# Turning half of the first queries behind the first scores, and hashing one pair ahead instead of two

## The chip, the cores and the metric

The kernel runs on one core of a Trainium2 chip. Its time is device time in microseconds (us), from launch to end. The time before is 871.74 us, the median of three runs (871.51 to 871.79). Times inside an execution come from one profiled execution, counted from the start of its span.

The engines of the core have short names in the profile: PE is the matrix engine, PEld its loading of weights, DVE is VectorE, ACT is ScalarE, POOL is GpSimd, and SP is SyncE, which here only issues DMAs. Every engine works through its own queue in order and waits at the head of it.

## What is computed

An attention whose mask comes from a hash, followed by a feed-forward block. The shapes are batch 4, heads 8, sequence 768, head size 64, and for the feed-forward 3072 tokens, 512 wide, 2048 inside. All inputs are 32-bit floats.

```python
# q, k, v: (4, 8, 768, 64); proj: (64, 6)
q_bits = (np.einsum('bhsd,dk->bhsk', q, proj) > 0).astype(np.int64)
k_bits = (np.einsum('bhsd,dk->bhsk', k, proj) > 0).astype(np.int64)
powers = 2 ** np.arange(n_bits)
q_bucket = np.sum(q_bits * powers, axis=-1)
k_bucket = np.sum(k_bits * powers, axis=-1)
mask = q_bucket[:, :, :, None] == k_bucket[:, :, None, :]
scores = scale * np.matmul(q, k.transpose(0, 1, 3, 2))
scores = np.where(mask, scores, -1000000000.0)
scores = scores - np.max(scores, axis=-1, keepdims=True)
attn = np.exp(scores)
attn = attn / (np.sum(attn, axis=-1, keepdims=True) + 1e-09)
attn_out = np.matmul(attn, v)
x = np.ascontiguousarray(attn_out.transpose(0, 2, 1, 3)).reshape(B * S, H * D)   # (3072, 512)
h = x @ w_in                                                                     # (3072, 2048)
g = h * (1.0 / (1.0 + np.exp(-1.702 * h)))
out = g @ w_out                                                                  # (3072, 512)
```

## The kernel before

**Tiling.** The attention works on 16 pairs of heads (`pairs`, numbered n = 0 to 15). The two heads of a pair, j = 0 and 1, lie on the upper and lower 64 partitions. The 768 queries are cut into two halves c = 0 and 1 of 384 (`HS`), and the 768 keys into six tiles of 128 (`kts`: `low` is the first three, `high` the last three, `every` all six).

**The steps of a pair**, with the lines of the kernel before:

- `fetch` (L317) loads k or q in blocks of 32 by 32 with four DMAs on SP's queue, `fetch_v` (L330) loads v with two. k and q have one buffer each, v has two.
- `turn` (L388) makes kT and qT from them, one VectorE transpose each (L391). `measure` (L393) takes the sum of squares on ACT, in the instruction that writes `junk` (L398).
- `hashed` (L402) multiplies kT and qT by the projection on PE, into one bank tagged "m". `featured` (L411) turns the signs into features f on VectorE (L413), and eight small DMAs on SP's queue spread them into kf and qf (L420). kf and qf exist twice, for even and odd pairs.
- `scores(n, c, kts)` (L423): for each key tile, PE adds the product of the features, which masks, to the product of kT and qT (L432), and ACT takes the exponential into e (L433). There are three score buffers in PSUM (`sps`, tag "s").
- `add_low` (L437): POOL adds the first three tiles of e, in two instructions (L440, L441), into acc0, which exists once. `add_high` (L443): VectorE adds the other three tiles and then acc0, in three instructions (L446, L448 twice). `total` (L477): PE sums over the keys (dn, L484).
- `values(n, c, kts)` (L450): PE multiplies e with v into an accumulator av (L463). `unload` (L471): ACT copies it into xT (L474, L475).
- `invert` (L486): VectorE turns dn (rt, L490), takes reciprocals (L493, L497) and turns them back (rs, L499). `norm` (L502): VectorE multiplies xT by them (L504).
- `convert` (L158), driven by `begin` and `step`: from pair 2 on, each pair also converts one chunk of `w_in` from its 64-bit form, with one load (raw, L162), six VectorE instructions (L178 to L198) and one on ACT (L190). The second VectorE step feeds the one on ACT.
- `x_sums`: pairs 12 to 15 each end with one sum over a part of xT on VectorE (L219 to L222), which the feed-forward needs.
- `guard` (L521): in the last pair, the largest of the sums of squares is found, on which a second, slower path depends (L998); with these inputs it is not taken.

**What sets the order.** For PE, VectorE, ACT and POOL the order of the program text is the order on the engine (`ORDERED`, L18). SP's queue is not in that set: a planner places its DMAs when the kernel is built, by its own costs, and each of them waits for its buffer to be free.

**Order around the change.** In `attention` the loop (L559) holds one pair per round. On PE a round is scores of both halves, values of both halves, the hash of pair n + 2 and dn. The keys and queries of pair n + 2 are turned between the two `add_high`, and the features of n + 2 are made after the conversion. k and q of pair n + 3 are fetched behind the first values.

**The first pair** has a path of its own (`first_pair`, L342). It loads its rows in another order and turns on PE: `turned` (L362) makes twelve matmuls with the identity for half of k or q (L366) into a score buffer and copies them out (L368); `bits` (L370) hashes one half on PE (L373) and writes the features on VectorE (L374). The keys' halves are copied by VectorE, the queries' by ACT. All of it comes ahead of the first scores but for the last `bits`, which is returned as `rest` and runs behind the first three score tiles.

**The accumulator av.** For c = 0 it lies in the pool `aps`, which dn uses too. For c = 1 it lies in a score buffer, except in pairs 0, 14 and 15, where it lies in the bank "m" (L454).

**The feed-forward** (from L693) follows with products of a Strassen form and a store of its middle result in DRAM. Its first product's parts are added on VectorE from L735 on.

Of the kernel before, what the change touches and what calls it, by code (L numbers as in the profile page):

```python
# [8 lines left out]
F32 = mybir.dt.float32  # L9
# [10 lines left out]
P = 128  # L20
# [18 lines left out]
def kernel(  # L39
# [17 lines left out]
    nc = tc.nc  # L57
# [10 lines left out]
    HS = HT * P  # L68
# [84 lines left out]
    for x in (0x3FFFFFFF, 0xFF800000):  # L153
        m = const.tile([P, 1], U32, name=f"mask_{x:x}")
# [128 lines left out]
    def attention(ff):  # L283
# [4 lines left out]
        with actx:  # L288
# [53 lines left out]
            def first_pair():  # L342


                b, hp = pairs[0]
                x = {}
                for i, (name, src) in enumerate((("k", k), ("q", q))):
                    raw = raws[0, name] = ld.tile([P, S // 32, 32], F32, tag=name, name=name)
                    x[name] = raw.rearrange("p s i -> p (s i)").rearrange("p (j t d) -> p j t d", j=2, d=D)
                    for j, queue in enumerate((nc.sync, nc.scalar)):  # L350
                        queue.dma_start(out=x[name][:, j], in_=src[b, 2 * hp + j].rearrange("(p t) d -> p t d", p=P))
                    if i == 0:
                        for j, queue in enumerate((nc.sync, nc.scalar)):
                            queue.dma_start(out=pj[D * j : D * (j + 1)], in_=proj)
                    xts[0, name] = wk.tile([P, S], F32, tag=f"{name}T", name=f"{name}T")

                nc.scalar.activation(const.tile([1, 1], F32, name="first"), ones[0:1, 0:1], Act.Exp)
                for _ in range(4):
                    nc.tensor.matmul(aps.tile([P, 512], F32, tag="av", name="warm"), idle[:, 0:P], idle, start=True, stop=True)  # L359
                hash_weights()  # L360

                def turned(name, c, move):  # L362
                    tp = sps.tile([P, 2, 512], F32, tag="s", name="tp")[:, 0, 0:HS]
                    for i in range(GT):
                        for j in range(2):
                            nc.tensor.matmul(tp[D * j : D * (j + 1), i * P : (i + 1) * P], x[name][:, j, c * GT + i, :], ident,  # L366
                                             start=True, stop=True)
                    move(xts[0, name][:, c * HS : (c + 1) * HS], tp)  # L368

                def bits(name, c):  # L370
                    cols = slice(c * HS, (c + 1) * HS)
                    h = sps.tile([P, 2, 512], F32, tag="s", name="hash0")[:, 0, 0:HS]
                    nc.tensor.matmul(h, pf0[name].rearrange("p j d -> p (j d)"), xts[0, name][:, cols], start=True, stop=True)  # L373
                    nc.vector.tensor_scalar(feats[0][name][:, cols], h, above0[name][:, 0:1], FEAT[name],  # L374
                                            op0=Alu.is_gt, op1=Alu.mult)

                measure(0, "k")
                turned("k", 0, nc.vector.tensor_copy)
                turned("k", 1, nc.vector.tensor_copy)
                turned("q", 0, nc.scalar.copy)  # L380
                turned("q", 1, nc.scalar.copy)
                measure(0, "q")
                bits("k", 0)
                bits("q", 0)
                bits("k", 1)
                return lambda: bits("q", 1)

            def turn(n, name):  # L388
                x = raws[n, name]
                xt = xts[n, name] = wk.tile([P, S], F32, tag=f"{name}T", name=f"{name}T")  # L390
                nc.vector.transpose(xt, x.rearrange("p s i -> p (s i)"))  # L391

            def measure(n, name):  # L393

                x = raws[n, name]
                i = 2 * n + "kq".index(name)
                junk = st.tile([P, S], BF16, tag="junk", name="junk", bufs=1)
                nc.scalar.activation(junk, x.rearrange("p s i -> p (s i)"), Act.Square, accum_out=sizes[:, i : i + 1])  # L398
# [24 lines left out]
            def scores(n, c, kts):  # L423
                qT, kT, qf, kf = xts[n, "q"], xts[n, "k"], feats[n % 2]["q"], feats[n % 2]["k"]
                cols = slice(c * HS, (c + 1) * HS)
                for kt in kts:
                    ps = sps.tile([P, 2, 512], F32, tag="s", name="ps")
                    keys = slice(kt * P, (kt + 1) * P)
                    for a, m, last in ((kf, qf, False), (kT, qT, True)):
                        for j in range(2):  # L430
                            hs = slice(D * j, D * (j + 1))
                            nc.tensor.matmul(ps[:, j, 0:HS], a[hs, keys], m[hs, cols], start=not last, stop=last)  # L432
                    nc.scalar.activation(es[c][:, kt, :, 0:HS], ps[:, :, 0:HS], Act.Exp, scale=1.0 / D**0.5)  # L433
# [16 lines left out]
            def values(n, c, kts):  # L450
                if 0 in kts:


                    if c and n == 0 or c and n + 2 > last:  # L454
                        avs[n, c] = mps.tile([P, HS + 1], F32, tag="m", name="av")
                    elif c:
                        avs[n, c] = sps.tile([P, 2, 512], F32, tag="s", name="av1")[:, 0, 0 : HS + 1]
                    else:
                        avs[n, c] = aps.tile([P, HS + 1], F32, tag="av", name="av")
                av, vt = avs[n, c], vts[n]  # L460
                for t in kts:
                    for j in range(2):
                        nc.tensor.matmul(av[D * j : D * (j + 1), :], vt[:, t, j, :], es[c][:, t, j, :],  # L463
                                         start=(t == 0), stop=(t == T - 1))
# [37 lines left out]
            def norm(n):  # L502
                x, rs = x_of(n), accs.pop(n)
                nc.vector.tensor_tensor(x, x, rs.rearrange("p (t s) -> p t s", t=T), op=Alu.mult)  # L504
# [8 lines left out]
            def begin(n):  # L513
                if 0 <= n - 2 < len(in_chunks) - LATE:
                    conv[n] = convert(cv, *in_chunks[n - 2])
                    step(n)
# [11 lines left out]


            low, high, every = range(GT), range(GT, T), range(T)  # L530
            rest = first_pair()
            fetch_v(0)
            for x in "kq":
                fetch(1, x)
            scores(0, 0, low)
            rest()
            add_low(0, 0)
            scores(0, 0, high)
            turn(1, "k")
            measure(1, "k")  # L540
            values(0, 0, low)
# [10 lines left out]
            fetch(2, "q")  # L552
            fetch_v(1)
            scores(0, 1, high)
            measure(2, "k")
            values(0, 1, low)
            values(0, 1, high)
            unload(0, 1)
            for n in range(1, last + 1):  # L559

                scores(n, 0, every)
                add_low(n, 0)
                if n == 1:
                    add_high(0, 1)
                    for x in "kq":
                        turn(2, x)
                    fetch(3, "k")
                    total(0)
                    measure(2, "q")
                    fetch(3, "q")  # L570
                    fetch_v(2)
                whole(invert(n - 1))
                norm(n - 1)
                if n == last:
                    guard(0)
                scores(n, 1, every)
                add_low(n, 1)
                add_high(n, 0)
                if n == 1:
                    hashed(2)  # L580
                    featured(2)
                if n + 2 <= last:
                    for x in "kq":
                        turn(n + 2, x)
                        measure(n + 2, x)
                if n == last:
                    guard(1)
                add_high(n, 1)
                values(n, 0, every)
                unload(n, 0)  # L590
                step(n, 6)
                if n + 3 <= last:
                    for x in "kq":
                        fetch(n + 3, x)
                if 1 < n < last:
                    fetch_v(n + 1)
                values(n, 1, every)
                unload(n, 1)
                if n + 2 <= last:
                    hashed(n + 2)  # L600
                total(n)
                if n + 2 <= last:
                    featured(n + 2)
                if n < last:
                    begin(n + 1)
                if n > last - len(x_sums):
                    x_sums[n - last - 1]()
# [378 lines left out]
    def whole(steps):  # L986
        for _ in steps:
            pass
# [46 lines left out]
```

## Time and profile before

| What | us |
|---|---|
| Median of three runs | 871.74 |
| The profiled execution's own time | 871.79 |
| Its span, first to last instruction | 869.9 |
| First scores | 10.81 |
| Attention's last dn ends, first product starts | 318.5 |
| PE busy from 60 to 262 (202 us) | 202.0 |
| VectorE busy in the same stretch | 191.7 |
| ACT busy in the same stretch | 139.0 |
| POOL busy in the same stretch | 67.7 |

The mean granted clock of PE is 0.997 of full speed over the span and 1.00 up to 700 us. The first two rows of the table are whole launches; the span leaves out about 1.9 us around the instructions. In a timeline line the columns are the start, the length, the engine, the source line, the operation, the tiles written and read, the shapes, the number of merged instructions, and, in brackets, how long the engine was idle before and who ended the wait. In the chain that ended last the columns are start, length, engine, tile and line. Line numbers are those of the kernel before; further down in the changed kernel they are a few lines lower.

### The profile page before, as it was taken

The page shows a single profiled execution, that of the slowest core. Times are in us where ns is not written, and L with a number is a line of the kernel's source. Part 1 is how long each engine was busy: PE and PEld are TensorE (multiplying, and loading weights), DVE is VectorE, ACT ScalarE, POOL GpSimd, SP SyncE. Part 2 cuts the span into 40 slices and gives each one's busy share as a digit, 9 for nine tenths or more (in the row PEclk, how much of TensorE's full clock was granted, in tenths as well). Part 3 has the DMA queues.
Part 4 walks back from the last instruction along what each step waited for, and adds up shares of the span by engine and source line. Part 5 has one row for each costly group of instructions (what it writes and reads, how often), then busy time and mean ns, then how long its engine had stood idle before and what let it go on. Part 6 is the DMA issues. An engine that isn't in the chain of part 4 may idle for free.

```text
span 869.9 us, 11937 instructions
## 1 busy us (share of the span) xinstructions
PE 859.7 (99%) x4077; PEld 502.2 (58%) x4077; DVE 722.4 (83%) x1020; ACT 313.4 (36%) x519; POOL 312.7 (36%) x275
## 2 busy tenths in 40 slices
PE   9999999999999999999999999999999999999996
PEld 5444444444444444444444444444888888888885
DVE  4589999999999897778777778888888977897786
ACT  5866667777666643322233222332000000000000
POOL 4242223334323466665544344659903100000000
PEclk9999999999999999999999999999999999999998
DMA  5536644445772204555555555575844685467524
GB/s 131 95 54 113 100 84 84 85 89 108 108 102 59 63 1 180 182 206 205 179 185 186 201 184 203 186 250 179 301 165 156 201 246 194 163 209 242 194 98 99
DMA packets 169156, 132.00 MB, mean 152 GB/s; under 512 B 123616, under 2 KB 138112, under 8 KB 163712
## 3 DMA queue, kind: packets, MB, share of 16 engines
q1 hardware_dynamic: 166528, 129.70, 52.2%
q10 hardware_dynamic: 2560, 1.46, 0.8%
q8 instruction: 34, 0.56, 0.3%
q14 instruction: 34, 0.28, 0.1%
HBM read 79.69 MB, written 50.33 MB: 149 GB/s over the span
## 4 chain that ended last, share of the span: by engine, by line
PE 96%; DVE 3%; issue 0%; ACTq 0%; ACT 0%; DVEq 0%
PE product L722 33%; PE product L834 26%; PE ps L432 18%; PE av L463 15%; PE hash L408 1%; PE dn L484 1%; DVE y L814 1%; DVE xT L838 1%; PE tp L366 1%; DVE t_x L838 0%; PE warm L359 0%; PE hash L373 0%; DVE t2a L221 0%; DVE raw_g L220 0%; DVE v L838 0%
## 5 line engine op out<-in xcount | busy, mean ns | idle before, releaser
L433 ACT ACTIVATE e<-ps 128x768 f32<-128x768 f32 x192 | 151.2, 812 | 28.1 <-PE ps L432 25.6
L432 PE MATMUL ps<-qT,kT 64*128 64x384 f32 x768 | 155.1, 482 | 0.0
L722 PE MATMUL product<-xT,w_in_sb 128*128 128x512 f32 x288 | 135.4, 592 | 0.0
L463 PE MATMUL av<-e,v 128*64 128x385 f32 x768 | 128.2, 488 | 0.0
L440 POOL TENSOR_TENSOR acc<-e 128x768 f32<-128x768 f32 x32 | 50.4, 1575 | 196.6 <-ACT e L433 177.1
L730 ACT ACTIVATE c<-c 128x512 f32<-128x512 f32 x72 | 45.3, 630 | 186.5 <-issue 78.6
L463 PEld LDWEIGHTS av<-e,v 128*64 128x64 f32 x768 | 53.7, 136 | 71.9 <-issue 70.4
L722 PEld LDWEIGHTS product<-xT,w_in_sb 128*128 128x128 f32 x288 | 54.6, 190 | 69.0 <-issue 64.5
L432 PEld LDWEIGHTS ps<-qT,kT 64*128 64x128 f32 x768 | 68.0, 187 | 38.6 <-issue 38.5
L722 PE MATMUL product<-t_x,s_in 128*128 128x512 f32 x192 | 90.2, 592 | 0.0
L219 POOL TENSOR_TENSOR v<-c,u 128x512 f32<-128x512 f32 x24 | 34.2, 1424 | 122.7 <-ACT c L730 122.7
L847 ACT COPY u<-product 128x256 f32<-128x256 f32 x21 | 7.8, 372 | 172.1 <-PE product L834 138.9
L722 PEld LDWEIGHTS product<-t_x,s_in 128*128 128x128 f32 x192 | 36.5, 190 | 45.9 <-issue 43.3
L432 PE MATMUL ps<-qf,kf 64*128 64x384 bf16 x384 | 62.8, 324 | 0.1
L441 POOL TENSOR_TENSOR acc<-acc,e 128x768 f32<-128x768 f32 x32 | 55.7, 1740 | 2.5
L446 DVE SCALAR_TENSOR_TENSOR acc<-e 128x768 f32<-128x768 f32 x32 | 48.8, 1524 | 5.1 <-ACT e L433 5.1
L722 PE MATMUL product<-xT,s_in 128*128 128x512 f32 x96 | 45.1, 592 | 0.0
L722 PE MATMUL product<-t_x,w_in_sb 128*128 128x512 f32 x96 | 45.1, 592 | 0.0
L432 PEld LDWEIGHTS <-kf 64*128 64x128 bf16 x384 | 18.9, 94 | 35.1 <-issue 6.1
L448 DVE TENSOR_TENSOR acc<-acc,e 128x768 f32<-128x768 f32 x32 | 34.4, 1075 | 3.3
L834 PE MATMUL product<-raw_g,xT 128*128 128x256 f32 x152 | 35.1, 379 | 0.0
L448 DVE TENSOR_TENSOR acc<-acc,acc 128x768 f32<-128x768 f32 x32 | 31.0, 969 | 4.8 <-POOL acc L441 1.6
(207 smaller groups left out, 1497.9 us busy)
## 6 DMA issues: line engine op xcount, KB each, us to landing
raw_g<-g_dram SPq DMA_DIRECT2D x22, 1024.0 KB
s_in<-g_dram SPq DMA_DIRECT2D x20, 1024.0 KB
g_dram<-c SPq DMA_DIRECT2D x72, 256.0 KB
g_dram<-t SPq DMA_DIRECT2D x48, 256.0 KB
raw<-in_moe_w_in_dram SPq DMA_DIRECT2D x16, 512.0 KB
raw<-in_moe_w_out_dram SPq DMA_DIRECT2D x16, 512.0 KB
v<-in_v_dram SPq DMA_DIRECT2D x32, 192.0 KB
g_dram<-u SPq DMA_DIRECT2D x24, 256.0 KB
```

The source lines that it names most:

```text
L219: return [lambda: eng.tensor_tensor(t1, b12, b11, op=Alu.subtract), lambda: eng.tensor_tensor(b12, b22, b12, op=Alu.subtract), lambda: eng ...
L366: nc.tensor.matmul(tp[D * j : D * (j + 1), i * P : (i + 1) * P], x[name][:, j, c * GT + i, :], ident, start=True, stop=True)
L432: nc.tensor.matmul(ps[:, j, 0:HS], a[hs, keys], m[hs, cols], start=not last, stop=last)
L433: nc.scalar.activation(es[c][:, kt, :, 0:HS], ps[:, :, 0:HS], Act.Exp, scale=1.0 / D**0.5)
L440: nc.gpsimd.tensor_tensor(acc, es[c][:, 0, :, 0:HS], es[c][:, 1, :, 0:HS], op=Alu.add)
L441: nc.gpsimd.tensor_tensor(acc, acc, es[c][:, 2, :, 0:HS], op=Alu.add)
L446: nc.vector.scalar_tensor_tensor(acc, e[0], T * TINY, e[1], op0=Alu.add, op1=Alu.add)
L448: nc.vector.tensor_tensor(acc, acc, x, op=Alu.add)
L463: nc.tensor.matmul(av[D * j : D * (j + 1), :], vt[:, t, j, :], es[c][:, t, j, :], start=(t == 0), stop=(t == T - 1))
L722: nc.tensor.matmul(ps, wq[LEFT[i]][:, kc, :], xq[RIGHT[i]][:, kc, :], start=(kc == 0), stop=(kc == K2 - 1))
L730: nc.scalar.activation(c, c, Act.Gelu_apprx_sigmoid)
L834: nc.tensor.matmul(ps, wq[LEFT[i]][:, c, :], gq[RIGHT[i]][:, c, :], start=(c == 0), stop=(c == F4 - 1))
```

## The change

The first pair: the second half of its queries is no longer turned ahead of the first scores. `first_pair` returns two steps. The first turns that half, with the copy on VectorE instead of ACT, and runs behind the first three score tiles. The second hashes it and runs behind the next three.

The other pairs: in round n the keys and queries of pair n + 1 (not n + 2) are turned, hashed and made into features. The keys are turned between the first step of `invert` and its reciprocals, the queries behind the second half's scores and ahead of `add_high(n, 0)`. The hash stands on PE between the scores and the values of the round. `norm(n - 1)` moves from behind `invert` to between the two `add_high`, in the last round behind both. The fetches of k and q of pair n + 2 stand at the end of the round. `measure` follows the hash. The accumulator of c = 1 lies in the bank "m" in every pair.

```diff
                 turned("q", 0, nc.scalar.copy)
-                turned("q", 1, nc.scalar.copy)
                 measure(0, "q")
 ...
-                return lambda: bits("q", 1)
+                return lambda: turned("q", 1, nc.vector.tensor_copy), lambda: bits("q", 1)
 ...
-                    if c and n == 0 or c and n + 2 > last:
-                        avs[n, c] = mps.tile([P, HS + 1], F32, tag="m", name="av")
-                    elif c:
-                        avs[n, c] = sps.tile([P, 2, 512], F32, tag="s", name="av1")[:, 0, 0 : HS + 1]
-                    else:
-                        avs[n, c] = aps.tile([P, HS + 1], F32, tag="av", name="av")
+                    pool, tag = (mps, "m") if c else (aps, "av")
+                    avs[n, c] = pool.tile([P, HS + 1], F32, tag=tag, name="av")
 ...
-            rest = first_pair()
+            rest_turned, rest_hashed = first_pair()
 ...
             scores(0, 0, low)
-            rest()
+            rest_turned()
             add_low(0, 0)
             scores(0, 0, high)
+            rest_hashed()
 ...
             scores(0, 1, high)
-            measure(2, "k")
 ...
                 if n == 1:
                     add_high(0, 1)
-                    for x in "kq":
-                        turn(2, x)
-                    fetch(3, "k")
+                    turn(2, "k")
                     total(0)
-                    measure(2, "q")
-                    fetch(3, "q")
-                    fetch_v(2)
-                whole(invert(n - 1))
-                norm(n - 1)
+                inverted = invert(n - 1)
+                next(inverted)
+                if 1 < n < last:
+                    turn(n + 1, "k")
+                whole(inverted)
 ...
                 scores(n, 1, every)
                 add_low(n, 1)
+                if n < last:
+                    turn(n + 1, "q")
                 add_high(n, 0)
-                if n == 1:
-                    hashed(2)
-                    featured(2)
-                if n + 2 <= last:
+                if n < last:
+                    hashed(n + 1)
+                    featured(n + 1)
                     for x in "kq":
-                        turn(n + 2, x)
-                        measure(n + 2, x)
-                if n == last:
+                        measure(n + 1, x)
+                else:
                     guard(1)
+                if n < last:
+                    norm(n - 1)
                 add_high(n, 1)
+                if n == last:
+                    norm(n - 1)
                 values(n, 0, every)
                 unload(n, 0)
                 step(n, 6)
-                if n + 3 <= last:
-                    for x in "kq":
-                        fetch(n + 3, x)
-                if 1 < n < last:
-                    fetch_v(n + 1)
                 values(n, 1, every)
                 unload(n, 1)
-                if n + 2 <= last:
-                    hashed(n + 2)
                 total(n)
                 if n + 2 <= last:
-                    featured(n + 2)
+                    for x in "kq":
+                        fetch(n + 2, x)
                 if n < last:
+                    fetch_v(n + 1)
                     begin(n + 1)
```

`measure` also takes its tile out of the table of loaded tiles (`raws.pop`), which changes no instruction.

More of the change, by code (lines that the diff above doesn't have):

```diff
@@ L393, in measure @@
             def measure(n, name):
-                x = raws[n, name]
+                x = raws.pop((n, name))
                 i = 2 * n + "kq".index(name)
@@ L577, in attention @@
                 add_low(n, 1)
+                if n < last:
+                    turn(n + 1, "q")
                 add_high(n, 0)
-                if n == 1:
-                    hashed(2)
-                    featured(2)
-                if n + 2 <= last:
+                if n < last:
+                    hashed(n + 1)
+                    featured(n + 1)
                     for x in "kq":
-                        turn(n + 2, x)
-                        measure(n + 2, x)
+                        measure(n + 1, x)
+                else:
+                    guard(1)
+                if n < last:
+                    norm(n - 1)
+                add_high(n, 1)
                 if n == last:
-                    guard(1)
-                add_high(n, 1)
+                    norm(n - 1)
                 values(n, 0, every)
```

## The prediction

> **What bounds the kernel now.** I read the page first (busy time, then the chain that ended last), then that chain in order of time, then the timelines of VectorE, POOL and SP over one pair.
>
> ```profile
> span 869.9 us, 11937 instructions
> PE 859.7 (99%) x4077; PEld 502.2 (58%) x4077; DVE 722.4 (83%) x1020; ACT 313.4 (36%) x519; POOL 312.7 (36%) x275
> PE 96%; DVE 3%; issue 0%; ACTq 0%; ACT 0%; DVEq 0%
> ```
>
> PE sets the end. The chain in order of time shows where it has a gap and what a pair costs:
>
> ```profile
> 10.14 0.63 DVE qf L374
> 10.81 2.60 PE ps L432 x18
> 13.41 0.84 PE hash L373 x2
> ...
> 145.92 0.78 PE hash L408 x8
> 146.71 0.65 PE dn L484 x8
> 147.35 9.80 PE ps L432 x72
> 157.15 7.92 PE av L463 x48
> ```
>
> From 10.81 to the end of attention at 318.52 PE never stops. A pair is 9.80 + 7.92 + 0.78 + 0.65 = 19.15 us. The same matmuls remain in the new kernel, so before 318.52 only the gap in front of 10.81 can shrink; anything else can only open gaps. I count time in a pair as T, with T = 0 where its scores begin (147.35 in the pair shown).
>
> VectorE is the second engine to watch. Its timeline in the same pair:
>
> ```profile
> 152.16 1.97 DVE L504 TENSOR_TENSOR xT<-xT,rs 128x768 f32<-128x768 f32 x1
> 154.05 0.94 DVE L446 SCALAR_TENSOR_TENSOR acc<-e 128x768 f32<-128x768 f32 x1
> ...
> 158.96 2.43 DVE L446 SCALAR_TENSOR_TENSOR acc<-e 128x768 f32<-128x768 f32 x1
> ...
> 163.43 0.69 DVE L178 SCALAR_TENSOR_TENSOR w_in_sb<-raw,mask_3fffffff 128x512 uint32<-128x512 uint32 x1
> ...
> 167.74 0.67 DVE L413 TENSOR_SCALAR f<-hash,above,weight 128x384 bf16<-128x384 f32 x1
> ```
>
> From one f (148.59) to the next (167.74) it works back to back: 19.15 us, too. In this are two stretched instructions, `norm` (L504, 1.89 us from start to next start, 1.0 where nothing overlaps it, at 268.13) and the first of `add_high` (L446, 2.54 against 1.05). Both times POOL's `add_low` is running (L441, 151.63 to 153.31 and 158.89 to 160.57), and VectorE finishes only after it. Without them the pair is 16.8 us of VectorE work.
>
> **Part 1, the start.** Half of the q turning (12 matmuls at L366, 24 in 2.19 us, so 1.09) leaves the front. Before, three hashes waited for it: qT's first half was copied at 7.93 to 8.41, but the q hash began only at 9.22, behind the k hash that PE could not start before 8.47. Now the k hash starts at about 7.45 and the q hash right after the copy, at 8.47, 0.75 sooner. With 0.96 us from hash to `bits` (8.47 to 9.43) and 0.62 for these, the first scores start at 10.1: 0.7 sooner. But the 1.09 us now stand between the scores, where PE had no gap: net +0.4. Its copy (L368, about 0.5 on VectorE) hides behind three score blocks (2.5 us). Bounds: -0.7 (if the turning found a gap) to +1.1 (if nothing is gained in front).
>
> **Part 2, one pair ahead instead of two.** Counts on PE, VectorE, ACT and POOL stay the same: 15 hashes, 15 f, 30 turns. What moves is order. On VectorE a pair is now rt, kT of n+1, reciprocals, rs, qT, add_high(n,0), f, norm, add_high(n,1), conversion. Two waits are new: kT for keys that were fetched only after the previous f, and f for a hash that PE issues at T = 9.8. Behind kT on VectorE stand the reciprocals, qT (which that hash needs) and add_high(n,0), which frees acc0 for POOL; behind f stand norm, add_high(n,1) (which dn needs) and the conversion. ACT's two squares keep their place behind the exponentials (T = 10.7 to 12.7), ahead of the unload due at 14.6.
>
> First the DMA loop. On SP's queue the fetches of k and q for n+2 now stand behind the eight feature DMAs of n+1, with raw and v behind them. The trace has this very sequence once:
>
> ```profile
> 49.39 1.47 SPq L420 DMA_DIRECT2D qf<-f  x2
> 50.98 3.05 SPq L328 DMA_DIRECT2D k<-in_k_dram  x4
> 54.14 2.16 SPq L328 DMA_DIRECT2D q<-in_q_dram  x4
> ```
>
> The eight begin at 44.79, so k is issued 6.2 us after f's end. When it lands I take from one-microsecond windows of DMA rate: 132, 62, 133, 161, 175 and 130 GB/s from 52 to 58, then 12. The 393 KB of k are through at 55.4, 4.4 us after issue, q's at 58.0.
>
> The Trainium skill (DMA: Bandwidth & Descriptors, Anatomy of one DMA — SWDGE (gpsimd) path) prices a DMA at about 2.0 us plus its bytes over 436 GB/s: for k an estimate of 2.9 us by that page, where the row has 4.4; by the page the loop below would be 1.5 us shorter and could not bind.
>
> The loop: f 0.6 + 0.1, features 6.2, k 4.4, kT 0.9, reciprocals 1.3, rs 1.1, qT 0.9, add_high 3.0, next f: 18.5 us against 19.15. So it holds, with 0.6 to spare: k lands at T = 3.0, add_high(n,0) ends at 10.2, and f waits for the hash until 10.8. Behind SP's waits, raw (T = 4.6, needed at 17) and v (needed at 10.6) still come in time.
>
> Second the collisions. add_high(n,0) frees acc0, and add_low(n,1) starts on POOL at 10.2 as f and then norm come due. How the two share is shown once, in pair 14:
>
> ```profile
> 291.34 2.23 POOL L440 TENSOR_TENSOR acc<-e 128x768 f32<-128x768 f32 x1 [3.96 <-DVE acc L448]
> 292.28 2.11 DVE L448 TENSOR_TENSOR acc<-acc,e 128x768 f32<-128x768 f32 x1
> 293.65 2.28 POOL L441 TENSOR_TENSOR acc<-acc,e 128x768 f32<-128x768 f32 x1
> ```
>
> VectorE waits for POOL's first instruction, gets in between (ends 294.39), POOL's second is stretched. So norm runs 11.8 to 12.6, L441 to 14.2, add_high(n,1) 14.2 to 17.2, conversion to 21.5 = T 2.35 of the next pair. dn needs add_high by 18.5: 1.3 spare. The conversion's third step frees ACT's L190 at 18.7, after which unload (0.75) ends at 20.2, and the next exponentials are due at 20.2 (T = 1.03): nothing spare. I take 0 for the twelve pairs between; bounds 0 and +0.4 each (if k lands 1 us later, or VectorE needs 0.2 more).
>
> Two places have no room. **Pair 1**: dn(0) ends at 36.95; rt, reciprocals, rs and qT (3.9) to 40.9, add_high to 43.9, f to 44.5; norm(0) waits for POOL until 45.5 and takes 1.3 (1.49 unhindered at 39.63); L441 to 48.45; add_high(1,1) to 51.45. PE wants its dn at 42.7 + 7.9 = 50.6: **+0.85**. Bounds 0 (no collision: add_high ends at 49.3) and +2. **Pairs 12 to 15** each add one sum over xT (1.14 us, 264.01 to 265.15). Two ahead, the slack took them; now they push everything later: conversion of pair 13 starts at 18.25, so exponentials of pair 14 start 1.0 late, three score buffers hide half, PE loses 0.5, and its dn waits 0.4 more; pair 15's exponentials start 1.2 late: 0.7. Sum **+1.6**; bounds 0 and +3.6 (three sums in full). After 318 VectorE ends about 0.7 later against PE than before; the first product's addition (L735) ran at 324.36 for a bank wanted back at 330.6, so that is covered. If VectorE were over 5 us later there, it would show.
>
> Each hash moves from the end of one pair into the middle of the next, which changes nothing in PE's sum (15 by 0.78). Also covered: the accumulator moved from the score buffers to the bank shared with the hash must wait for f (11.4) by T = 14.5.
>
> **Sum.** 0.4 + 0.85 + 0 + 1.6 = +2.85 on the profiled execution's own 871.79 us (span 869.9 plus 1.9 around it), 0.05 above the median of 871.74: **874.6 us**.
>
> **Rivals.** *The loop binds*: k, delayed 1 us, makes every pair follow VectorE and SP: 11 pairs at +0.4 on top, 879. For it: q waited 2.5 us of VectorE at 35.55, and the same transfers beside raw data took 4.8 us (158.86 on); against it, nothing else is in flight at that time now. *No change*: one mechanism, the meeting of norm and POOL's add_low. If norm is not held there, VectorE's pair falls by 2 us; add_high(1,1) ends before 50.6, the last sums fit, and only the start's +0.4 is left: 872.1. It decides as soon as norm is held less than 0.7 us. For it: no row has this meeting; against it: both stretched rows, in every pair. *Faster*: the 0.7 us in front without the 1.09 behind: 871.0, still within 0.2%; PE's unbroken chain excludes more, unless the phase after 318 gains, whose code is the same.
>
> **How the numbers follow.** Forecast 0.50 (own range 873.2 to 876), the loop 0.27, no change 0.18, faster 0.05. A measurement here can tell 0.2%, 1.7 us. Low end 872.1 is the case of no change, high end 879.0 the loop's. Slower takes nearly all of the forecast and all of the loop, 0.76; same the no-change case, most of the fast one and the forecast's edge, 0.21; faster 0.03.
>
> **What would show it.** First scores near 10.1 and, from there, +0.4 at the first values. PE waiting for acc (L448) before dn of pair 1, near 51. Pairs 3 to 12 at 19.15; if they show 19.3 to 19.6 instead, kT waiting for k means the loop, ACT's L190 means the conversion. norm stretched to about 1.5 to 2 us with POOL's L440 beside it. Pairs 14 and 15 longer by 0.5 to 1. Wrong if PE stands nowhere between 10.1 and 318, or if products after 318 move by more than attention did.

## The result, and the profile after

The changed kernel takes 874.27 us, the median of six runs (873.80 to 874.98), against 871.63 us of six runs of the kernel before (871.17 to 871.79). The ratio is 1.0031 with a 95% interval of 1.0018 to 1.0044: slower by 0.3%, 2.6 us. The forecast was 874.6. The total is right; two of its four terms are not, and they happen to cancel. One run of the kernel before, on the chip of the last two experiments, took 907.53 us at a granted clock of 0.947 in place of 0.996 to 0.998 and is left out of every ratio.

The profiled execution of the changed kernel took 874.98 us. Its page, in the lines that answer to those of before:

```profile
span 873.1 us, 11818 instructions
PE 862.2 (99%) x4077; PEld 501.7 (57%) x4077; DVE 720.5 (83%) x1021; ACT 311.5 (36%) x518; POOL 321.3 (37%) x275
PE 96%; DVE 2%; DMA 1%; issue 0%; SPq 0%; ACTq 0%; ACT 0%; DVEq 0%
```

PE has the same 4077 matmuls and still sets the end, but is busy for 862.2 us in place of 859.7. VectorE is busy for less, 720.5 in place of 722.4. PE's busy time does not tell work from waiting here: from 50 to 53, where one wait lies, it is 3.00 us of 3. Behind the first product the two executions take the same, 551.4 us (318.52 to 869.9) and 551.5 (321.59 to 873.1), so the difference lies ahead of it. The chain in order of time (start, length, engine, tile, line) says where:

```profile
10.57 2.60 PE ps L432 x18
...
50.79 1.49 PE dn L479 x8
...
147.89 0.78 PE dn L479 x8
148.67 9.80 PE ps L432 x72
158.47 0.78 PE hash L408 x8
159.25 7.92 PE av L458 x48
167.17 0.78 PE dn L479 x8
```

Pair 1's dn takes 1.49 where a dn takes 0.78: that is the wait which was forecast. `norm` and the first of `add_high` run against POOL, the sums end at 51.39, and the second half of dn's weights is loaded only then (timeline):

```profile
44.43 2.61 DVE L499 TENSOR_TENSOR xT<-xT,rs 128x768 f32<-128x768 f32 x1
45.69 2.76 POOL L441 TENSOR_TENSOR acc<-acc,e 128x768 f32<-128x768 f32 x1
46.88 2.38 DVE L446 SCALAR_TENSOR_TENSOR acc<-e 128x768 f32<-128x768 f32 x1
50.43 0.96 DVE L448 TENSOR_TENSOR acc<-acc,acc 128x768 f32<-128x768 f32 x1
51.44 0.14 PEld L479 LDWEIGHTS dn<-acc,ones 128*32 128x32 f32 x4 [0.58 <-DVE acc L448]
```

After it a pair is 9.80 + 0.78 + 7.92 + 0.78 = 19.28 us, against 19.15 before. The 0.13 us are in dn, the same eight matmuls: 0.65 in the kernel before, 0.78 here. This is no wait for the sums: in pairs 2 to 15 they are ready 0.20 to 1.43 us before dn's first weight load (in the pair shown below, 165.81 against 167.09). The chain of the kernel before has a dn of 0.78, too, in pair 14, where no hash stands ahead of it:

```profile
299.04 0.78 PE dn L484 x8
```

PE's weight loads show what differs. First the kernel before, where the hash (128*32, as dn) stands ahead of dn; then the changed kernel, where values (128*64) do. The profile labels the matmuls by 128*32, 128*64 or 64*128, which I call their shape. Columns are start, length, engine, line, operation, tiles, shape, number, and the idle time ahead.

```profile
146.20 0.13 PEld L484 LDWEIGHTS dn<-acc,ones 128*32 128x32 f32 x4 [0.19 <-issue]
146.53 0.13 PEld L484 LDWEIGHTS dn<-acc,ones 128*32 128x32 f32 x4 [0.19 <-issue]
```

```profile
147.82 0.16 PEld L479 LDWEIGHTS dn<-acc,ones 128*32 128x32 f32 x8 [0.60 <-issue]
```

Before, the first four loads start 0.51 us ahead of dn's place in the chain (146.71), while the hash still runs. After, all eight start only when the values are through. That the late loads are the whole of the 0.13 us is not shown.

The Trainium skill (TensorEngine Tiling (Array Packing), Tiling Modes, Key Properties) states it as a rule: a change of the tiling mode, not of the tile alone, drains the TensorE. The rows agree with it, and the price here is 0.13 to 0.14 us.

A pair had three changes of shape before (scores, values, hash and dn together) and has four now (scores, hash, values, dn). This concerns the 13 pairs in which a hash stood beside dn before, 1 to 13: 13 times 0.13 to 0.14 gives 1.7 to 1.8 us. From the first values to the last dn the kernel before takes 301.0 us (16.78 to 317.74), the changed one 303.5 (17.35 to 320.81): +2.5, which is 0.71 of waiting in pair 1 and 1.8 in the shapes.

VectorE in the steady pair, from the timeline of the changed kernel:

```profile
159.32 0.68 DVE L413 TENSOR_SCALAR f<-hash,above,weight 128x384 bf16<-128x384 f32 x1 [0.49 <-PE hash L408]
159.91 1.42 DVE L499 TENSOR_TENSOR xT<-xT,rs 128x768 f32<-128x768 f32 x1
161.25 2.43 DVE L446 SCALAR_TENSOR_TENSOR acc<-e 128x768 f32<-128x768 f32 x1
...
164.85 0.96 DVE L448 TENSOR_TENSOR acc<-acc,acc 128x768 f32<-128x768 f32 x1
```

And POOL in the same place:

```profile
158.97 1.54 POOL L440 TENSOR_TENSOR acc<-e 128x768 f32<-128x768 f32 x1 [4.34 <-DVE acc L448]
160.59 2.27 POOL L441 TENSOR_TENSOR acc<-acc,e 128x768 f32<-128x768 f32 x1
```

`norm` (L499) meets POOL's `add_low` as forecast, and L441 is stretched from 1.68 to 2.27. But VectorE has room: f waits 0.49 us for the hash, and in eight of the pairs between 60 and 262 kT waited for k, 3.7 us in all.

### The profile page after: what moved, and what is told of

The parts are those of the page before. It is cut to its first block, busy times and chain, and to the rows that moved or that the text cites. A ratio compares the mean times of both kernels' runs of the same rounds, so it can differ in the third digit from the quotient of the medians.

```text
span 873.1 us, 11818 instructions
## 1 busy us (share of the span) xinstructions
PE 862.2 (99%) x4077; PEld 501.7 (57%) x4077; DVE 720.5 (83%) x1021; ACT 311.5 (36%) x518; POOL 321.3 (37%) x275
## 4 chain that ended last, share of the span: by engine, by line
PE 96%; DVE 2%; DMA 1%; issue 0%; SPq 0%; ACTq 0%; ACT 0%; DVEq 0%
PE product L713 33%; PE product L825 27%; PE ps L432 18%; PE av L458 15%; PE dn L479 2%; PE hash L408 1%; DVE xT L829 1%; DMA q<-in_q_dram 1%; DVE y L805 1%; PE hash L373 0%; PE tp L366 0%; DVE v L829 0%; DVE t2a L221 0%; DVE raw_g L220 0%; ACTq L812 0%
## 5 line engine op out<-in xcount | busy, mean ns | idle before, releaser
L440 POOL TENSOR_TENSOR acc<-e 128x768 f32<-128x768 f32 x32 | 51.3, 1603 | 192.6 <-ACT e L433 96.5
L441 POOL TENSOR_TENSOR acc<-acc,e 128x768 f32<-128x768 f32 x32 | 64.0, 2001 | 2.5
L446 DVE SCALAR_TENSOR_TENSOR acc<-e 128x768 f32<-128x768 f32 x32 | 50.6, 1580 | 4.0 <-ACT e L433 4.0
L432 PEld LDWEIGHTS <-kf 64*128 64x128 bf16 x384 | 19.3, 94 | 34.9 <-issue 10.8
L448 DVE TENSOR_TENSOR acc<-acc,e 128x768 f32<-128x768 f32 x32 | 31.8, 995 | 3.3
```

Of the source, the lines that this page charges most:

```text
L440: nc.gpsimd.tensor_tensor(acc, es[c][:, 0, :, 0:HS], es[c][:, 1, :, 0:HS], op=Alu.add)
L441: nc.gpsimd.tensor_tensor(acc, acc, es[c][:, 2, :, 0:HS], op=Alu.add)
L446: nc.vector.scalar_tensor_tensor(acc, e[0], T * TINY, e[1], op0=Alu.add, op1=Alu.add)
L448: nc.vector.tensor_tensor(acc, acc, x, op=Alu.add)
```

## The experiments

Each kernel is compared with runs of the kernel before on the same chip. The medians of those were 871.58 us for the first four kernels (18 runs), 871.71 for `e6_k_later` (7 runs) and 871.49 for the last two (15 runs).

**The first pair alone.** The kernel before, with the changed first pair.

```diff
-                turned("q", 1, nc.scalar.copy)
-                return lambda: bits("q", 1)
+                return lambda: turned("q", 1, nc.vector.tensor_copy), lambda: bits("q", 1)
...
             scores(0, 0, low)
-            rest()
+            rest_turned()
             add_low(0, 0)
             scores(0, 0, high)
+            rest_hashed()
```

> The kernel before with the first pair's edit alone (half of q turned behind the first scores). The forecast's term for the start was +0.4 us, that is 872.0. What the trace of the changed kernel suggests instead: there the first scores began 3.4 us after q's load released PE (7.15 to 10.57), before it was 4.5 (6.35 to 10.81), and the first values 10.2 after it against 10.4; so the edit itself is worth -0.2 (871.4), and the +0.6 seen at the first values was q landing 0.85 later in that execution. In this profile: first values at q's landing plus 10.2 if so, plus 10.8 if the forecast's term holds. Pairs 2 to 13 at 19.14.

Measured: 871.9 us (871.16 to 872.44, 11 runs), 1.0004 of before (0.9995 to 1.0014): no difference. The executions differ by up to 1 us in when the first queries land, so the start has to be read from that point, the first turning of q. From there to the first scores the old start took 4.46, 4.55 and 3.79 us (the three profiled kernels that have it), the new one 3.37, 3.81, 3.16, 4.13, 4.19 and 3.81 (all six): means of 4.27 and 3.75, so about 0.5 are gained in front. From the first scores to the first values the old one takes 5.97, the new one 6.78 us: 0.81 are lost there. By the means the edit is worth +0.3, but single executions of one start lie up to 1 us apart, so its size is not known better than that. In this kernel the first values come 10.6 us after the first turning of q, between the 10.2 and 10.8 that were expected, and dn of pair 1 takes 0.87 in place of 0.65.

**The loop alone.** The changed kernel with the first pair of the kernel before (the diff above, reversed).

> The changed kernel with the old first pair, so the one-pair-ahead loop alone. Theory A (PE pays for one more change of matmul shape in each of 13 pairs, 0.13 each, because the hash no longer stands beside dn, and for one wait of dn in pair 1, 0.7): +2.4, 874.0, pairs 2 to 14 at 19.28, no PE wait but in pair 1. Theory B (as forecast: waits for VectorE in pairs 1 and 13 to 15, none in the middle): pairs 3 to 12 at 19.15, 14 and 15 longer by 0.9 and 0.7. Theory C (the middle's 0.14 is a hidden wait for k or for the exponentials): 874.0 as well, which the next run tells apart.

Measured: 875.99 us (874.57 to 876.34, 5 runs), 1.0045 (1.0032 to 1.0059). That is 2 us above what was expected. The profile shows pairs of 19.28, as expected, but two places that the changed kernel does not have, and 0.9 us behind the first product, where the code is the same. One place is in pair 1: the second `add_high` ends at the same time of the span as in the changed kernel, though PE is 0.4 us earlier, because VectorE waited 0.53 us for an exponential. The other is at the start of pair 4. ACT there:

```profile
91.58 0.69 ACT L190 ACTIVATE raw<-raw 128x512 f32<-128x512 f32 x1 [4.58 <-DVE bits L182]
...
92.82 9.15 ACT L434 ACTIVATE e<-ps 128x768 f32<-128x768 f32 x12
```

ACT stands in front of L190 until VectorE's conversion has got that far, the unload stands behind it, and the exponentials start 1.71 us after the pair's scores (91.11) in place of 1.03. From dn to dn this is 19.75 us in place of 19.28, with 0.27 of the difference in the dn ahead. So the chain from conversion to exponentials that the prediction feared exists. That the rest of the 2 us is more than scatter between executions is not shown.

**Two more changes of shape, and nothing else.** The kernel before, with the hash put between the two halves of the values.

```diff
                 values(n, 0, every)
                 unload(n, 0)
...
-                values(n, 1, every)
-                unload(n, 1)
                 if n + 2 <= last:
                     hashed(n + 2)
+                values(n, 1, every)
+                unload(n, 1)
                 total(n)
```

> The kernel before, still two pairs ahead, with the hash moved from between the values and dn to between the two halves of the values. No transfer and no VectorE work changes its place. Theory A (0.13 for each additional change of matmul shape, here two more in a pair: back to the values, and from these to dn): pairs 1 to 13 at 19.40, total +3.4, 875.1. Theory C (the middle of the changed kernel is slower by a wait on k, VectorE or ACT, not by PE's own order): pairs at 19.14, total unchanged at 871.6.

Measured: 875.29 us (874.75 to 875.92, 4 runs), 1.0043 (1.0027 to 1.0058). The chain of this kernel:

```profile
139.03 4.03 PE av L463 x24
143.07 0.78 PE hash L408 x8
143.85 4.03 PE av L463 x24
147.88 0.78 PE dn L484 x8
```

The values take 2 by 4.03 = 8.06 in place of 7.92, dn 0.78 in place of 0.65: two more changes of shape, 0.14 and 0.13 us. The pair is 19.43. No DMA and no instruction was added; the order on PE alone costs 3.7 us, more than the whole change under study.

**Pair 1 without the meeting.** The changed kernel, with `norm(0)` of pair 1 behind the second `add_high`.

```diff
-                if n < last:
+                if 1 < n < last:
                     norm(n - 1)
                 add_high(n, 1)
-                if n == last:
+                if n in (1, last):
                     norm(n - 1)
```

> The changed kernel, with norm(0) in pair 1 moved behind add_high(1,1), out of the way of POOL's add_low(1,1). If the meeting of norm and add_low makes dn of pair 1 wait (forecast 0.85, measured 0.7 in the changed kernel's trace), dn follows the values at once: 0.7 less than the changed kernel, about 873.6, and the chain's dn of pair 1 shrinks from 1.49 to 0.78. If add_high(1,1) is late for another reason (rt of pair 0 comes late), dn stays at 1.49 and the time at 874.3.

Measured: 873.93 us (873.1 to 874.48, 8 runs), 1.0026 (1.0015 to 1.0036). From the chain:

```profile
49.69 0.78 PE dn L479 x8
...
69.78 2.53 PE ps L432 x18
```

dn of pair 1 waits no more: 0.71 us are gone there, by moving one VectorE instruction out of POOL's way. About 0.3 of them come back: the pair whose scores start at 69.78, with a gap of 0.02 behind their first three tiles, takes 19.50, one later 19.38. From the first values to the last dn this kernel takes 0.4 us less than the changed one, about what the medians show (0.34), though their intervals overlap.

**The DMA loop's room.** The changed kernel, from pair 3 on with two of the eight feature DMAs issued a second time.

```diff
                             queue.dma_start(out=feats[n % 2][x][...], in_=f[r0 : r0 + 2 * NB, :])
+                            if n > 2 and c == 1 and x == "q":
+                                queue.dma_start(out=feats[n % 2][x][...], in_=f[r0 : r0 + 2 * NB, :])
```

> The changed kernel with two of the eight feature DMAs of each pair from 3 on issued a second time (the same data to the same place), which puts the fetch of k 1.45 us later in SP's queue. In the changed kernel's steady pair f waits 0.49 us for the hash after the work that k released, so the loop from f over features, k, kT, reciprocals, rs, qT and add_high to the next f takes 18.8 us of 19.28. Theory A (the loop is real and its room is that small): 18.8 + 1.45 = 20.25, so 12 pairs get 0.97 longer, +11.6 us: 886, with PE waiting in each pair; by the forecast's own 18.5 us it would be +0.67 each and 882. Theory B (k's landing is set by the transfers and not by its place in the queue, or VectorE makes the time up): pairs stay at 19.28 to 19.4, 874.3 to 875.5.

Measured: 882.82 us (882.37 to 884.16, 4 runs), 1.0127 (1.011 to 1.0144): about 8.5 us more than the changed kernel. The chain of waits leaves PE and goes round the loop (the added DMAs are L423 here):

```profile
112.52 0.74 SPq L423
113.35 0.73 SPq L423
...
114.69 2.80 DMA k<-in_k_dram
...
117.61 0.98 DVE kT L391
```

The pairs take 19.3 to 21.1 us, 19.95 on average from pair 1 to pair 14 (50.62 to 310.00), against 19.33 in the changed kernel (50.72 to 302.04). So 1.45 us more on SP's queue cost 0.62 a pair: the loop has room for about 0.8 of them and no more. The forecast's 18.5 us for the loop, which gives 0.67 a pair and 882, fits this better than the 18.8 of Theory A.

**An instruction more on VectorE.** The changed kernel, with a copy that nobody reads behind the second `add_high` of pairs 2 to 14.

```diff
                 add_high(n, 1)
+                if 1 < n < last:
+                    filler = st.tile([P, S], BF16, tag="junk", name="filler", bufs=1)
+                    nc.vector.tensor_copy(filler.rearrange("p (j s) -> p j s", j=2), es[1][:, GT + 2, :, 0:HS])
```

> The changed kernel with one more VectorE instruction of about 1.0 us (a copy of 128x768 that nobody reads) behind the second add_high of pairs 2 to 14: what the sums over xT of the last three pairs put there, now in all. Theory A (VectorE's idle time of 15.6 us in 10.5 pairs, 1.5 a pair, takes it): pairs stay at 19.28 to 19.35, 874.3 to 875.2. Theory B (the forecast's account: the exponentials behind the conversion have nothing spare, so each instruction of 1 us makes PE lose about 0.5): pairs of 19.7 to 19.9, 13 of them, 880 to 882, with PE waiting for a score buffer at the fourth block of scores and ACT's exponentials beginning at T = 2.0 in place of 1.03.

Measured: 877.77 us (876.73 to 878.50, 4 runs), 1.0070 (1.0054 to 1.0085), between the two theories. The copy took 0.55 us and not 1.0. (It writes into the tile of `junk`; a tile of its own would leave 39.375 KB of a partition for tiles that need 42.125.) Of the pairs from 2 to 13 three are 0.04 to 0.24 longer, the others stay at 19.28: the room in VectorE takes it. But pairs 14 and 15, which come behind two and three of the sums over xT, get 0.60 and 1.91 us longer. In pair 14, 0.2 of it are late exponentials and 0.4 a hash that waits for qT; the sum ahead of qT (L220) meets POOL there and takes 2.57 us, in the changed kernel 1.22. ACT at the start of pair 15, first in the changed kernel (the pair's scores begin at 302.89):

```profile
302.91 0.68 ACT L190 ACTIVATE raw<-raw 128x512 f32<-128x512 f32 x1 [3.87 <-DVE bits L182]
304.15 9.41 ACT L433 ACTIVATE e<-ps 128x768 f32<-128x768 f32 x12
```

then with the copy:

```profile
306.35 0.68 ACT L190 ACTIVATE raw<-raw 128x512 f32<-128x512 f32 x1 [6.04 <-DVE bits L182]
307.57 9.15 ACT L433 ACTIVATE e<-ps 128x768 f32<-128x768 f32 x12
```

Only part of the 1.91 us belongs to the exponentials. The second half of pair 14's dn starts 1.26 us after the first (303.31), as it waits for the sums that VectorE now ends later, and the scores of pair 15 begin behind it, at 305.41:

```profile
304.57 0.84 PE L479 MATMUL dn<-acc,ones 128*32 128x384 f32 x4 [0.42 <-DVE acc L448]
```

This wait is 1.25 us. The other 0.66 are the exponentials: they cost PE nothing when they start 1.26 us after the pair's scores (pair 15 of the changed kernel), 0.2 at 1.7 (pair 7 of this kernel) and 0.66 at 2.16 (pair 15).

**dn beside the hash.** The changed kernel, with each dn moved to the next pair, right behind the hash there, and VectorE's work on it behind f; the second `add_high` comes after the conversion. All but the last dn lie in a score buffer, and rs takes the place of an acc that is no longer needed (a third buffer for acc would leave as little room as the tile of the last experiment).

```diff
-                inverted = invert(n - 1)
-                next(inverted)
...
-                whole(inverted)
...
                 if n < last:
                     hashed(n + 1)
+                    total(n - 1)
                     featured(n + 1)
...
+                whole(invert(n - 1))
                 if n < last:
                     norm(n - 1)
-                add_high(n, 1)
+                else:
+                    add_high(n, 1)
...
                 step(n, 6)
+                if n < last:
+                    add_high(n, 1)
                 values(n, 1, every)
                 unload(n, 1)
-                total(n)
...
+            total(last)
```

> The changed kernel (874.27) with each dn but the last moved from the end of its pair to the next pair, right behind the hash there (both 128*32 matmuls), so that values stand directly ahead of the next scores. The matmuls and their number stay the same; VectorE's order of a pair becomes kT, qT, add_high(n,0), f, rt, reciprocals, rs, norm, conversion, add_high(n,1). Theory A (a change of matmul shape costs PE 0.13 us, and the changed kernel has one more of them in each pair): the chain shows dn at 0.65 behind the hash, pairs of 9.80 + 0.78 + 0.65 + 7.92 = 19.15 in place of 19.28, 14 times 0.13 = -1.8 us, and dn of pair 1 without a wait, -0.7: 871.8, from 871.2 to 872.6. Theory B (0.78 is what a dn costs for another reason than what stands ahead of it, and the pairs' 0.13 comes from VectorE or the DMA loop): pairs stay at 19.28, only the wait in pair 1 goes: 873.5. If the score buffer that dn takes, or the later second add_high, holds PE up, it waits for rt or for an exponential, and the time lies above 874.

Measured: 872.05 us (870.96 to 872.53, 11 runs), 1.0006 of before (0.9997 to 1.0015). The chain:

```profile
138.34 7.92 PE av L458 x48
146.26 9.80 PE ps L432 x72
156.06 0.78 PE hash L408 x8
156.84 0.65 PE dn L479 x8
```

dn is back at 0.65 and the pair at 19.14 us, from the first dn to the fourteenth, with no wait in pair 1. Theory A had 871.8. The wait in pair 1 and the added changes of shape are both removed, and it is level with the kernel before. No version here was faster than that.

## Why the prediction was right, and where it was not

**The start (+0.4).** Both halves of the step are there: about 0.5 us sooner in front (0.7 forecast), and the turning now between the scores, 0.81 us and not 1.09. Both are smaller than forecast, and the term is about +0.3, within a scatter that is as large.

**Pair 1 (+0.85).** Right in place, cause and nearly in size: 0.71 us in front of dn. Moving `norm(0)` out of the meeting removed it.

**The pairs between (0).** This is the step that failed. "The same matmuls remain in the new kernel" is true, but the conclusion that "each hash moves from the end of one pair into the middle of the next, which changes nothing in PE's sum" is not. The sum took a matmul's price as its own, when it depends on what stands ahead. Next to the hash dn costs 0.65, behind values 0.78. The kernel before showed both prices in its chain, in pairs 0, 14 and 15 against the rest, and the difference was passed over. The term is 1.7 to 1.8 us. The order moved on the kernel before (+0.28 a pair) and the order mended in the changed one (-0.14 a pair) show it from both sides.

The rest of that step held. The DMA loop did not bind, and its 0.6 us of room was sized well: 0.49 in the row of f, about 0.8 by the added DMAs. So the rival of the binding loop was near: two small DMAs more in each pair and it would have come true.

**Pairs 12 to 15 (+1.6).** The mechanism exists, as the added copy shows, but the term is 0: pairs 14 and 15 take 19.28 and 18.70 us, as the shapes alone make them. Forecast were exponentials 1.0 and 1.2 us late; measured they start 1.02 and 1.26 us behind the scores, against 1.03 in a steady pair, so on time and 0.23 late. "Nothing spare" was wrong twice. VectorE's waits for k and for the hash are room that takes most of a sum of 1.13 us: the f of pair 14's features waits only 0.17 for the hash, that of pair 15's not at all.

```profile
274.99 0.68 DVE L413 TENSOR_SCALAR f<-hash,above,weight 128x384 bf16<-128x384 f32 x1 [0.17 <-PE hash L408]
294.49 0.67 DVE L413 TENSOR_SCALAR f<-hash,above,weight 128x384 bf16<-128x384 f32 x1
```

And PE does not notice exponentials that are a little later: in pairs 3 to 6 of the changed kernel they start up to 0.4 us later than in a steady pair, and all dn of these pairs stand 19.28 apart.

**The rivals.** "No change" had `norm` meet POOL for less than 0.7 us. The meeting is there, and PE waits 0.71 us for it, but only in pair 1; its 872.1 misses that wait and the 1.8 us of the shapes, which no case had. "Faster" rested on 0.7 us in front, of which about 0.5 are real, without the turning behind, which costs 0.8.

In sum, the steps as measured are 0.3 + 0.7 + 1.8 + 0 = 2.8 us, the medians differ by 2.64, and the forecast was 0.4 + 0.85 + 0 + 1.6 = 2.85. That it came so near is luck: 1.8 us that it did not have stand in for 1.6 that it had.

## What to carry to other kernels

Where PE sets the end, count the changes of matmul shape along its order, not only the matmuls, and look in the chain for the same group at two prices: what stands ahead of it is the difference. A busy share of 100% does not exclude a wait, as the dn of pair 1 shows. Room on a second engine is read from what it waits for in a steady round; a sum of its busy times leaves it out. A loop through several queues is worth adding up link by link, since a little more in one link (1.45 us of issue here) then costs every round.

## What the runs showed of the hardware

A change between 128*64 and 128*32 matmuls costs PE 0.13 to 0.14 us, in both directions; the kernel with the hash between the values pays both.

The stretching of VectorE beside POOL depends on the instruction. In the kernel with dn beside the hash VectorE is busy for 168.5 us of the stretch from 60 to 262, against 186.4 in the changed kernel, with the same 1021 VectorE instructions in the whole span. Its timeline, while POOL runs L441 from 157.99 to 159.68:

```profile
158.51 0.92 DVE L492 RECIPROCAL r<-rt 32x12 f32<-32x12 f32 x4
...
160.48 0.96 DVE L499 TENSOR_TENSOR xT<-xT,rs 128x768 f32<-128x768 f32 x1
```

The reciprocals, with one input, keep their duration beside POOL (0.92 also at 37.75 in the kernel with the loop alone, where POOL is idle), while `norm`, with two, took 1.27 to 2.00 us in pairs 2 to 14 of the changed kernel, where it met POOL, and takes 0.96 behind it (`norm(0)`, in pair 1, 2.61 and 1.58). The Trainium skill (SBUF — State Buffer, SBUF: two separate sides) has this as an exclusive lock on a port pair that VectorE's instructions with two SBUF inputs and POOL's share. The rows of the changed kernel agree: POOL's L440 ends at 160.51, `norm` 0.8 us after it, L441 1.5 after `norm`, and L446 0.8 after L441, each of them started before the one ahead had ended. The 18 us saved on VectorE brought no time: PE was full.
